# All output stores on one queue, the last evictions between ScalarE and VectorE swapped, and new instruction orders, in a transducer joint kernel

## The chip, the cores and the metric

The kernel runs on one core of a Trainium2 chip. A core has a matrix engine (TensorE, PE in the profile), which reads its weights by a separate instruction (PEld); a vector engine (VectorE, DVE); a scalar engine (ScalarE, ACT); GpSimd (POOL); and SyncE (SP), which here does nothing but issue transfers. Engines take their instructions in order and wait for each other through semaphores. The metric is the device time in microseconds of one execution; the lower the better.

## The reference

Two strided five-tap convolutions with a gelu after each, two projections, a tanh over every pair of time step and label step, and an output projection:

```python
h = sum_i einsum("btc,cd->btd", xp[:, i:i+T], w1[i])       # x is 2 x 4000 x 512, 5 taps
h = gelu(h)[:, ::2]                                         # 2 x 2000 x 512
f = sum_i einsum("btc,cd->btd", hp[:, i:i+T1], w2[i])
f = gelu(f)[:, ::2]                                         # 2 x 1000 x 512
fe = f @ w_f;  ge = g @ w_g                                 # g is 2 x 8 x 512
j = tanh(fe[:, :, None, :] + ge[:, None, :, :])             # 2 x 1000 x 8 x 512
out = j @ w_o                                               # 2 x 1000 x 8 x 512, bf16
```

The last product is the largest: 16,000 rows of 512 by a 512 x 512 matrix, with one tanh for each of its 8.2 million inputs.

## The kernel before

**Convolutions.** Each convolution computes three neighbouring outputs from products of sums and differences of inputs and of weights, so that there are fewer products (`Triple`, `Unit`, steps `s1` to `s5`). The sums of the inputs ("planes", "r", "t2" and so on) are made by VectorE, with some scalings by ScalarE or VectorE (`scaled`, lines 608 and 609); the weight sums are made in `w1part` and `w2part`. A `Unit` is one block of 128 output channels. TensorE has the products, ScalarE moves accumulators out (`sd`, `hT`, `fT`, line 451), VectorE combines (lines 602 and 446).

**The joint stage**, from about 130 us on. The 16,000 rows are 125 tiles of 128. Four neighbouring tiles by all 512 columns are taken as a 2 x 2 block product with seven products in place of eight (class `Seven`, 28 of them, methods `p1` to `p7`): four sums of the tanh values go to `ss` (method `sums`, line 1091, each 128x512, VectorE or GpSimd), four products are kept in `sn` (method `keep`, lines 560 on ScalarE and 561 on VectorE) or added to what was kept while they are moved out to `og` (line 446 on VectorE). The remaining tiles are direct products (class `Plain`), moved out to `ost`. The tanh itself runs on ScalarE, 1,000 columns at a time, into the rings `jT` and `jX` (line 451), ahead of the products. The convolution work of the second batch is mixed into the first part of this stage.

**Evictions.** `evict(None, ...)` may be done by ScalarE or VectorE: it is a "flex" operation, whose engine is the one in whose order list its number stands. The four sums of a `Seven` are flex too, between VectorE and GpSimd.

**Order.** All operations are numbered as the program makes them (0 to 1644). `ORDER` holds, for each engine, the list of its operations' numbers, written as differences from one to the next. A planner (`Plan`) works out from the tiles which operation must wait for which, and emits each engine's list in its order with the waits. So a change of `ORDER` moves work in time and, for flex operations, between engines; what is computed stays.

**Stores.** `store` and `store2` write finished tiles to HBM (lines 1037 and 1027), all from SyncE's queue but two at the end, issued by ScalarE.

**The end.** The last `Seven` is tiles 118 to 121. Behind its product 3 come, in TensorE's order: product 7, the plain tile 122, the first 384 columns of tile 124, product 4, tile 123 in two halves of 256 columns (method `halves`), and the last 128 columns of tile 124. The four last evictions and stores:

```python
for t, eng in ((2 * r, "act"), (2 * r + 1, "sp")):     # Seven.stores(1, True): tiles 120 and 121
Plain(plains[1]).halves("dve", "sp")                    # tile 123
end.part(slice(3 * P, NT), "act", "act")                # tile 124, last 128 columns
```

So ScalarE evicts product 4 into `og`, issues the store of tile 120, evicts the last 128 columns, and issues their store; the instructions stand in this order in its list.

Of the kernel before, what the change touches and what calls it, by code (L numbers as in the profile page):

```python
# [12 lines left out]
P = 128  # L13
# [2 lines left out]
ORDER = {  # L16
    "pe": """
# [13 lines left out]
        1 6 3 3 1 4 2 3""",  # L31
    "act": """
# [8 lines left out]
        91 -68 101 -95 96 -83 -8 25 -3 32 -23 25 -36 16 8 3 14 6 5 9 3 10 6 21 -8 14 10 3 10 6 10 3 8 6 6 3 12 7 1 8 1""",  # L41
    "dve": """
# [9 lines left out]
        -13 19 18 74 -52 -13 20 16 -9 6 -27 43 7 6 2 19 -7 13 15 -3 9 8 2""",  # L52
    "pool": """
        1 42 1 -42 1 1 1 15 218 1 -217 258 -252 253 8 89 174 150 1 54 -2 1 -31 33 33 2 -1 38 -36 35 40 -38 37 34 2 33
        -32 33 32 -30 31 1 1 33 1 28 1 1 28 155 -154 1 27 2 -1 33 -31 32 1 28 2 -1 31 -29 30 1 26 37 -36 37 1 1 33 34
        -33 34 -32 33 1 29 2 -1 33 2 -1 33 -31 32 1 34 2 35 2 27 -26 27 1 1 24 1 28 -26 29""",
    "sp": """
        6 2 1 1 1 1 1 1 1 1 1 1 1 2 2 1 1 1 1 2 1 1 1 1 1 248 1 1 1 1 1 1 2 1 1 1 1 1 254 1 1 145 3 33 33 4 1 1 30 4 33
        4 1 1 33 4 31 4 1 1 29 4 29 4 1 1 29 4 25 4 1 1 25 4 25 4 1 1 27 4 27 4 1 1 25 4 25 4 1 1 19 1 11 4 21 11 4 19
        11 4 17 11 1 1 4 17 11 1 1 4 17 11 4 1 1 19 11 4 21 1 11 4 25 4 23 1 1 4 23 4 19 1 1 7 3 3 5 5""",  # L60
}


# [252 lines left out]
def bass_standalone__seq2seq_rnn_t_joint__speech_kernel(  # L316
# [36 lines left out]
    NT = 512  # L353
# [4 lines left out]
    with ExitStack() as es:  # L358
# [659 lines left out]
        def store2(jt, src, key):  # L1018
            lo = jt * P
            if lo // T2 != (lo + 2 * P - 1) // T2:  # L1020
                for t in range(2):
                    store(jt + t, lambda a, b, t=t: src(a, b, t), key)
                return
            b, u, t = lo // T2 // U, lo // T2 % U, lo % T2
            s = src(0, P, slice(0, 2))
            dst = out[b, t:t + 2 * P, u, :].rearrange("(t p) d -> p t d", p=P)
            pl.dma("sp", lambda e: e.dma_start(dst, s.ap), (s,), (), sem_of(key), 4 * P * P * 4)

        def store(jt, src, key, eng="sp", cl=slice(0, NT)):
            lo = c0 = jt * P  # L1030
            while lo < c0 + P:
                vv = lo // T2
                n = min((vv + 1) * T2, c0 + P) - lo
                b, u, t = vv // U, vv % U, lo % T2
                s = src(lo - c0, lo - c0 + n)
                dst = out[b, t:t + n, u, cl]
                pl.dma(eng, lambda e, s=s, dst=dst: e.dma_start(dst, s.ap), (s,), (), sem_of(key), 2 * n * P * 4)  # L1037
                lo += n
# [30 lines left out]
        class Seven:  # L1069
# [60 lines left out]
            def stores(self, r, split=False):  # L1130
                key = ("s", self.n % len(og), r)
                if not split:
                    store2(self.jt + 2 * r, lambda a, b, t: self.o.rows(a, b, 2 * r + t if isinstance(t, int) else slice(2 * r, 2 * r + 2)), key)
                    return
                for t, eng in ((2 * r, "act"), (2 * r + 1, "sp")):
                    store(self.jt + t, lambda a, b, t=t: self.o.rows(a, b, t), key + (eng,), eng)

            def p1(self):
# [94 lines left out]
        plains = [j for j in range(ntile) if not any(q <= j < q + 4 for q in jts)]  # L1233
# [5 lines left out]
        for i, q in enumerate(seven):  # L1239
# [3 lines left out]
            r = []  # L1243
# [25 lines left out]
        end = Plain(plains[2])  # L1269
        end.part(slice(0, 3 * P), "dve", "sp")  # L1270
        seven[-1].p4(True)
        Plain(plains[1]).halves("dve", "sp")
        end.part(slice(3 * P, NT), "act", "act")

        pl.emit(block, [(s[0], s[1]) for s in sems.values()])

# [27 lines left out]
```

## Time and profile before

| | |
|---|---|
| median of 3 runs | 252.02 us (251.9 to 252.15) |
| profiled execution, its own time | 251.77 us |
| its span, first to last instruction | 249.9 us |
| granted TensorE clock | 0.999 |
| PE / PEld busy | 243.4 us / 182.9 us |
| DVE / ACT / POOL busy | 207.8 / 196.8 / 100.6 us |
| HBM read / written | 7.60 MB / 16.38 MB |

The page of the profile gives the busy time of each engine, then the same in 40 slices of 6.25 us; the chain that ended last follows the execution back from its end, at each step to what released it. The timeline lists single instructions, merged where they follow each other, with the idle time before them in brackets. An instruction is written as its tiles, out<-in. `SPq` and `ACTq` are the issuing of transfers by these engines, which does not count as busy time. One busy share hides something here: two evictions that follow each other on an engine overlap, so what one more of them costs is the distance of their starts and not their duration.

### The profile page before, as it was taken

How to read it: one execution, taken by the hardware profiler on the slowest of the kernel's cores; microseconds unless marked ns; L12 is line 12 of the kernel's file. 1: busy time of each engine (PE TensorE's matmuls, PEld its weight loads, DVE VectorE, ACT ScalarE, POOL GpSimd, SP SyncE). 2: the span in 40 equal slices, each digit the busy share in tenths (PEclk: the TensorE clock that was granted, in tenths of full speed). 3: DMA queues.
4: the chain of work that ended last, by engine and by line, in shares of the span. 5: the costliest groups of instructions: out<-in, count | busy, mean ns of one | idle time of the engine just before them, and what ended most of it. 6: DMA issues, size and time to landing. Idle time of an engine off the chain costs nothing.

```text
span 249.9 us, 5265 instructions
## 1 busy us (share of the span) xinstructions
PE 243.4 (97%) x1938; PEld 182.9 (73%) x1944; DVE 207.8 (83%) x369; ACT 196.8 (79%) x338; POOL 100.6 (40%) x107
## 2 busy tenths in 40 slices
PE   7999999999999999999999999999999999999992
PEld 3979976666666666666557887777888877878872
DVE  1799996967999993996857989769999999996962
ACT  4787868458795575533799999999999999997661
POOL 1000000000000000000008998969899999998510
PEclk9999999999999999999999999999999999999999
DMA  7999999999000070000001142232453656455465
GB/s 243 295 216 180 175 182 172 188 161 357 8 3 0 0 244 12 0 3 0 1 3 42 64 150 84 88 111 99 147 171 122 198 160 211 132 192 163 146 204 165
DMA packets 54871, 31.83 MB, mean 127 GB/s; under 512 B 31902, under 2 KB 54590, under 8 KB 54846
## 3 DMA queue, kind: packets, MB, share of 16 engines
q1 hardware_dynamic: 54558, 31.34, 47.7%
q8 instruction: 15, 0.25, 0.5%
q10 hardware_dynamic: 288, 0.16, 0.2%
q14 instruction: 10, 0.08, 0.1%
HBM read 7.60 MB, written 16.38 MB: 96 GB/s over the span
## 4 chain that ended last, share of the span: by engine, by line
PE 88%; ACT 5%; DMA 2%; DVE 1%; issue 1%; ACTq 1%; SPq 0%; DVEq 0%
PE acc L459 88%; ACT jT L451 2%; DMA w_sb<-in_w_dram 2%; ACT og L560 1%; ACT sn L560 1%; ACT jX L451 1%; ACTq L1037 1%; DVE og L446 1%; DVE sn L561 0%; DVE og L561 0%; PE acc L596 0%; SPq L486 0%; ACT ost L451 0%; DVEq L277 0%; ACTq L277 0%
## 5 line engine op out<-in xcount | busy, mean ns | idle before, releaser
L446 DVE TENSOR_TENSOR og<-acc,sn 128x512 bf16<-128x512 f32 x84 | 54.9, 680 | 6.6 <-PE acc L459 6.4
L451 ACT ACTIVATE jT<-feT,geT 128x1000 bf16<-128x1000 f32 (+5 forms) x60 | 57.4, 1015 | 0.3 <-DVE feT L446 0.3
L1091 POOL TENSOR_TENSOR ss<-jT 128x512 f16<-128x512 bf16 x34 | 39.4, 1176 | 35.2 <-DVE ss L1091 33.4
L459 PE MATMUL acc<-tw,ss 128*128 128x256 f16 x336 | 46.4, 273 | 0.0
L459 PE MATMUL acc<-row,w_sb 128*128 128x334 bf16 (+2 forms) x224 | 39.0, 297 | 0.0
L459 PEld LDWEIGHTS acc<-tw,ss 128*128 128x128 f16 x336 | 32.4, 98 | 7.5 <-ACT sn L560 0.5
L459 PE MATMUL acc<-wo_sb,jT 128*128 128x256 bf16 (+1 forms) x205 | 33.3, 283 | 0.2
L560 ACT ACTIVATE sn<-acc 128x512 f32<-128x512 f32 x49 | 30.3, 626 | 3.0 <-PE acc L459 2.8
L451 ACT ACTIVATE hT<-acc 128x334 bf16<-128x334 f32 (+3 forms) x36 | 15.4, 432 | 16.6 <-PE acc L459 16.0
L459 PEld LDWEIGHTS acc<-row,w_sb 128*128 128x128 bf16 x224 | 21.3, 97 | 9.2 <-DVE acc L602 0.7
L561 DVE COPY sn<-acc 128x512 f32<-128x512 f32 x35 | 23.8, 683 | 4.5 <-PE acc L459 4.2
L451 ACT ACTIVATE sd<-acc 128x334 f32<-128x334 f32 (+2 forms) x48 | 20.6, 432 | 6.3 <-PE acc L459 4.9
L459 PEld LDWEIGHTS acc<-wo_sb,jT 128*128 128x128 bf16 x208 | 20.3, 98 | 5.0
L443 POOL MEMSET hT<- 128x8 bf16 (+2 forms) x6 | 0.8, 148 | 55.2 <-ACT hT L451 42.9
L1091 POOL TENSOR_TENSOR ss<-ss,jT 128x512 f16<-128x512 f16 x18 | 21.0, 1172 | 2.7 <-DVE ss L1091 2.3
L1091 POOL TENSOR_TENSOR ss<-jT,ss 128x512 f16<-128x512 bf16 x17 | 20.0, 1177 | 2.1 <-DVE ss L1091 2.1
L446 DVE TENSOR_TENSOR row<-row 128x1336 bf16<-128x1336 bf16 (+2 forms) x24 | 18.9, 803 | 0.0
L602 DVE SCALAR_TENSOR_TENSOR acc<-acc,sd 128x334 f32<-128x334 f32 (+2 forms) x24 | 11.7, 486 | 8.1 <-PE acc L459 8.0
L451 ACT ACTIVATE jX<-feT,geT 128x1000 bf16<-128x1000 f32 (+3 forms) x20 | 18.2, 956 | 0.0
L459 PE MATMUL acc<-xp,w_t 128*128 128x334 bf16 (+1 forms) x96 | 17.6, 305 | 0.0
L459 PE MATMUL acc<-hT,w_t 128*128 128x334 bf16 x96 | 17.6, 304 | 0.0
L459 PE MATMUL acc<-wo_sb,ss 128*128 128x256 bf16 x112 | 17.3, 273 | 0.0
(130 smaller groups left out, 469.7 us busy)
## 6 DMA issues: line engine op xcount, KB each, us to landing
out_dram<-og SPq DMA_DIRECT2D x42, 256.0 KB, 2.2
w_sb<-in_w_dram SPq DMA_DIRECT2D x10, 512.0 KB, 5.9
out_dram<-og SPq DMA_DIRECT2D x14, 128.0 KB, 2.0
out_dram<-ost SPq DMA_DIRECT2D x10, 128.0 KB, 2.0
xr<-in_x_dram SPq DMA_DIRECT2D x1, 512.0 KB, 3.6
wf_sb<-in_w_f_dram SPq DMA_DIRECT2D x1, 512.0 KB, 4.1
wg_sb<-in_w_g_dram SPq DMA_DIRECT2D x1, 512.0 KB, 5.2
wo_sb<-in_w_o_dram SPq DMA_DIRECT2D x1, 512.0 KB, 7.6
```

Of the source, the lines that this page charges most:

```text
L443: pl.op("pool", lambda e: e.memset(v.ap, 0.0), (), (v,))
L446: pl.op(eng, lambda e: e.tensor_tensor(out=o.ap, in0=a.ap, in1=b.ap, op=op), (a, b), (o,), 0.02 + 2.14e-3 * o.ap.free_size() if eng == "po ...
L451: pl.op("act", lambda e: e.activation(o.ap, i.ap, func, scale=scale, bias=0.0 if bias is None else bias.ap), rd, (o,), o.ap.free_size() * ...
L459: ins = e.matmul(o.ap, lhsT=l.ap, rhs=r.ap, start=start and n == 0, stop=stop and n == len(pairs) - 1, skip_group_check=not check)
L560: pl.flex({"act": (lambda e: e.activation(o.ap, v.ap, ACT.Copy), 0.05 + n * 0.833e-3), "dve": (lambda e: e.tensor_copy(out=o.ap, in_=v.ap) ...
L561: "dve": (lambda e: e.tensor_copy(out=o.ap, in_=v.ap), 0.065 + n * 1.04e-3)}, (v,), (o,))
L602: pl.op(eng, lambda e: e.scalar_tensor_tensor(out=o.ap, in0=a.ap, scalar=f, in1=b.ap, op0=ALU.mult, op1=add), (a, b), (o,), vec_cost(o, (a ...
L1037: pl.dma(eng, lambda e, s=s, dst=dst: e.dma_start(dst, s.ap), (s,), (), sem_of(key), 2 * n * P * 4)
L1091: fn = lambda e, o=S[i], x=x, y=y, op=op: e.tensor_tensor(out=o.ap, in0=x.ap, in1=y.ap, op=op)
```

## The change

1. `Seven.stores(1, True)`: the store of tile 120 is issued by SyncE, ahead of that of tile 121.
2. Tile 123's two halves are evicted by ScalarE, not VectorE; the store stays with SyncE.
3. Tile 124's last 128 columns are evicted by VectorE, not ScalarE, and stored by SyncE, not ScalarE. ScalarE issues no transfer any more.
4. `ORDER` is new for all five engines. TensorE's list has another operation at 101 of its 696 places, the first at the 59th; SyncE's differs only in its last four entries. The flex operations that change engines, counted by number from the two lists: in the joint stage 24 evictions of 128x512 go from VectorE to ScalarE and 16 the other way, 18 sums go from GpSimd to VectorE and 16 the other way; in the convolutions five scalings go from ScalarE to VectorE and three small ones the other way.

```diff
 ORDER = {
     "pe": """
...
-        15 1 -6 1 14 1 7 1 8 -12 -12 1 12 5 1 12 -5 1 5 2 1 2 1 8 1 4 1 -8 20 19 -29 3 1 16 19 25 -47 1 -17 20 19 -28 1
+        15 1 -6 1 14 1 -8 1 14 1 2 -6 1 6 7 -2 3 4 1 2 1 2 1 8 5 -7 8 -5 17 -10 29 -26 1 16 19 -22 1 46 -63 20 19 -28 1
...
     "act": """
...
-        91 -68 101 -95 96 -83 -8 25 -3 32 -23 25 -36 16 8 3 14 6 5 9 3 10 6 21 -8 14 10 3 10 6 10 3 8 6 6 3 12 7 1 8 1""",
+        42 -24 26 -21 8 3 42 2 -24 -9 14 8 3 44 -37 13 -11 1 24 3 -26 42 -10 23 -93 101 6 10 3 10 6 10 3 8 6 6 3 12 7 4
+        2""",
...
     "sp": """
...
-        11 4 17 11 1 1 4 17 11 1 1 4 17 11 4 1 1 19 11 4 21 1 11 4 25 4 23 1 1 4 23 4 19 1 1 7 3 3 5 5""",
+        11 4 17 11 1 1 4 17 11 1 1 4 17 11 4 1 1 19 11 4 21 1 11 4 25 4 23 1 1 4 23 4 19 1 1 7 3 3 4 1 5 3""",
 }
...
-                for t, eng in ((2 * r, "act"), (2 * r + 1, "sp")):
+                for t, eng in ((2 * r, "sp"), (2 * r + 1, "sp")):
                     store(self.jt + t, lambda a, b, t=t: self.o.rows(a, b, t), key + (eng,), eng)
...
         seven[-1].p4(True)
-        Plain(plains[1]).halves("dve", "sp")
-        end.part(slice(3 * P, NT), "act", "act")
+        Plain(plains[1]).halves("act", "sp")
+        end.part(slice(3 * P, NT), "dve", "sp")
```

More of the change, by code (lines that the diff above doesn't have):

```diff
@@ L23 @@
         -5 1 8 43 1 -39 1 12 -8 1 10 -8 1 20 1 2 1 2 1 16 -7 1 2 1 4 6 1 2 1 2 1 2 1 2 1 6 1 2 1 3 1 5 1 4 1 2 1 2 1 2 1
[7 rows of a table removed]
-        1 6 3 3 1 4 2 3""",
-    "act": """
[8 rows of a table removed]
-        91 -68 101 -95 96 -83 -8 25 -3 32 -23 25 -36 16 8 3 14 6 5 9 3 10 6 21 -8 14 10 3 10 6 10 3 8 6 6 3 12 7 1 8 1""",
-    "dve": """
[9 rows of a table removed]
-        -13 19 18 74 -52 -13 20 16 -9 6 -27 43 7 6 2 19 -7 13 15 -3 9 8 2""",
[7 rows of a table added]
+        -11 1 12 1 2 1 2 1 8 1 -4 1 6 3 3 1 4 2 3""",
+    "act": """
[9 rows of a table added]
+        2""",
+    "dve": """
[9 rows of a table added]
+        19 42 -15 3 -13 21 -2 18 6 3 6 7 7 14 -7 6 3 20 6 -13 16 18 -7 13 15 -3 9 13""",
     "pool": """
-        1 42 1 -42 1 1 1 15 218 1 -217 258 -252 253 8 89 174 150 1 54 -2 1 -31 33 33 2 -1 38 -36 35 40 -38 37 34 2 33
-        -32 33 32 -30 31 1 1 33 1 28 1 1 28 155 -154 1 27 2 -1 33 -31 32 1 28 2 -1 31 -29 30 1 26 37 -36 37 1 1 33 34
-        -33 34 -32 33 1 29 2 -1 33 2 -1 33 -31 32 1 34 2 35 2 27 -26 27 1 1 24 1 28 -26 29""",
+        1 42 1 -42 1 1 1 15 218 1 -217 258 -252 253 8 89 174 150 22 33 -2 1 2 33 2 35 -34 35 40 -2 35 -34 35 -33 69 31
+        -32 34 -32 33 32 2 27 -26 27 1 1 28 2 -1 154 -125 1 31 2 -1 30 2 -1 30 -28 29 1 1 26 37 -36 37 -35 36 1 33 2 -1
+        33 2 -1 31 2 -1 33 2 -1 33 2 -1 37 -1 36 -34 36 1 26 2 -1 2 53 -28 29 -27 29""",
     "sp": """
```

48 rows, old and new, of the table ORDER are left out of this document.

## The prediction

> **What bounds the kernel now.** I read the page first: busy time by engine, and the slices.
>
> ```profile
> span 249.9 us, 5265 instructions
> PE 243.4 (97%) x1938; PEld 182.9 (73%) x1944; DVE 207.8 (83%) x369; ACT 196.8 (79%) x338; POOL 100.6 (40%) x107
> ...
> PE   7999999999999999999999999999999999999992
> ...
> ACT  4787868458795575533799999999999999997661
> ```
>
> PE is busy in every slice but parts of the first and the last. Its instructions stay the same, so the body can hardly get shorter; it can only get longer, where a new order lets PE wait. ScalarE is full from about 130 us to 220 us. The second view is the chain that ended last, its final pieces (start us, us, what):
>
> ```profile
> 223.56 18.78 PE acc L459 x163
> 242.34 0.05 issue
> 242.39 1.91 PE acc L459 x11
> 244.30 0.02 issue
> 244.32 0.60 ACT og L560
> 244.93 0.02 issue
> 244.95 2.44 ACTq L1037
> 247.39 0.04 issue
> ...
> 247.50 0.28 ACT ost L451
> ```
>
> Up to 244.3 us the chain is PE's work. Then it leaves PE and runs through ScalarE: the eviction of product 4, the issue of its store, which takes 2.44 us, and the last small eviction behind it. The timeline of that stretch shows what the others had done by then:
>
> ```profile
> 244.12 1.26 PE L459 MATMUL acc<-wo_sb,jX 128*128 128x256 bf16 x12
> ...
> 244.76 0.86 DVE L565 CAST ost<-acc 128x256 bf16<-128x256 f32 x2 [0.32 <-PE acc L459]
> 244.94 0.38 SPq L1037 DMA_DIRECT2D out_dram<-og  x1
> ...
> 245.65 0.33 SPq L1037 DMA_DIRECT2D out_dram<-ost  x1
> 247.50 0.28 ACT L451 ACTIVATE ost<-acc 128x128 bf16<-128x128 f32 x1 [2.58 <-DMA out_dram<-ost]
> 247.80 0.34 ACTq L1037 DMA_DIRECT2D out_dram<-ost  x1
> ```
>
> PE has ended at 244.12 + 1.26 = 245.38. The last 128 columns lie ready from then on, and are touched at 247.50 because ScalarE is still issuing. From the last issue to the end of the span it is 249.9 - 247.80 = 2.1 us. So 4.5 us lie behind PE's end, about 2.1 of them idle for one long issue.
>
> **The end, part by part.** The stores of the tile `og` (count, then ns min/median/max) price an issue:
>
> ```profile
> L1027 SPq DMA_DIRECT2D out_dram<-og x42: 372/394/502, 141.2 to 243.4; - x42
> L1037 SPq DMA_DIRECT2D out_dram<-og x40: 318/418/2207, 143.1 to 244.9; - x40
> ...
> L1037 ACTq DMA_DIRECT2D out_dram<-og x1: 2444/2444/2444, 244.9 to 244.9; - x1
> ...
> DMA to landing us min/median/max: 1.5/2.1/4.3
> ```
>
> The new end, step by step, with PE's end held:
> - Product 4's eviction stays on ScalarE, 244.32 to 244.92.
> - Tile 123's halves: the first is ready at 244.76 (VectorE began there, released by PE). ScalarE's evictions of 512 columns follow each other at about 0.48 us (rows below), so the first half starts at 244.80. No row has 256 columns on ScalarE; 128 take 0.28 us and 512 take 0.60, so 256 lie between and I take 0.39 by proportion. The second half is ready some 0.44 us after the first (half of VectorE's 0.86, which went with PE), runs from about 245.2 to 245.6.
> - The last 128 columns on VectorE, freed of the halves, start at 245.4. Their price lies under the 0.43 of a half; at 0.28, as on ScalarE, they are out at 245.7. Cover: this and the halves end side by side, and a store of SyncE's queue is still ahead of both.
> - SyncE gets two more issues, and both stand in front of or behind others. Tile 120: 244.94 to 245.32. Tile 121, which started at 244.94, now 245.34 to 245.72. Tile 123 waited for its halves until 245.65 and now starts at about 245.75. The last 128 columns follow at 245.75 + 0.33 = 246.1.
> - From there 2.1 us as before: the end is at 248.2, against 249.9. **The gain is 1.7 us.**
>
> Bounds of this term: with issues of 0.33 and a landing 0.1 shorter, 248.0 (gain 1.9); with issues of 0.50 (the largest of the 42) and a landing that queues behind three 128 KB stores, 2.5 us, it is 249.1 (gain 0.8). The new waits have little behind them: behind SyncE's wait for tile 123 stands only the last store, and behind ScalarE's halves nothing.
>
> Here a rule of the Trainium skill speaks against the change. The page "DMA: Bandwidth & Descriptors", section "Issuing engines are not separate DMA queues", says that transfers started from several engines run on the same 16 DMA engines, so that a second queue saves only the time of issuing. By it, giving up the second queue buys nothing and costs one issue of 0.38 us: 252.4 us. The two rows at 244.94 and 244.95 disagree: the same kind of store, 0.38 us on SyncE and 2.44 us on ScalarE, side by side. I go by the rows.
>
> **The body.** Stages by 10 us (PE, PEld, DVE, ACT, POOL busy), and rows that price a moved eviction:
>
> ```profile
> 10.00:30.00 20.00, 20.00 (x217) 17.79 (x215) 19.82 (x50) 17.54 (x37) 0.48 (x4) 1.00 1.09 203
> ...
> 200.00:210.00 10.00, 9.95 (x81) 7.92 (x82) 9.54 (x16) 10.00 (x14) 10.00 (x10) 1.00 0.57 183
> 210.00:220.00 10.00, 9.95 (x82) 7.82 (x81) 10.00 (x18) 10.00 (x14) 10.00 (x9) 1.00 0.47 154
> 220.00:230.00 10.00, 9.95 (x84) 7.96 (x83) 7.83 (x14) 8.98 (x18) 9.30 (x9) 1.00 0.56 180
> 230.00:240.00 10.00, 10.00 (x94) 8.60 (x92) 8.67 (x14) 7.00 (x14) 5.97 (x6) 1.00 0.51 168
> ```
>
> ```profile
> 198.62 2.47 DVE L446 TENSOR_TENSOR og<-acc,sn 128x512 bf16<-128x512 f32 x4
> ...
> 221.78 0.68 ACT L560 ACTIVATE ost<-acc 128x512 bf16<-128x512 f32 x1
> 222.25 0.69 ACT L560 ACTIVATE sn<-acc 128x512 f32<-128x512 f32 x1
> ...
> 223.83 0.83 ACT L451 ACTIVATE jX<-feT,geT 128x152 bf16<-128x152 f32 x2
> ...
> 230.10 1.15 POOL L1091 TENSOR_TENSOR ss<-jX 128x512 f16<-128x512 bf16 x1
> ```
>
> On ScalarE two evictions start 222.25 - 221.78 = 0.47 us apart, on VectorE (2.47 - 0.68) / 3 = 0.60. Of the moved evictions 24 go to ScalarE and 16 away: net 8, or 8 x 0.48 = 3.8 us more for ScalarE and 4.8 less for VectorE, which takes two more sums. The cover is ScalarE's idle time from 220 to 240 us, 20 - 8.98 - 7.00 = 4.0 us. The evictions that were issued from 200 to 222 us give 11 to ScalarE and 2 away: 9 x 0.48 = 4.3 us, in a stretch where ScalarE is full. It then runs its tanhs later: the last ended at 223.83 + 0.83 = 224.7 us, and the sums that use the last tiles were made at 230.1, so 5.4 us were to spare. Net of 1.1 us, it holds; that is thin but enough. SyncE's stores in the body keep their order.
>
> The convolutions move five scalings to VectorE, where 10 to 30 us is 19.82 of 20 us full, and three small ones to ScalarE:
>
> ```profile
> 15.47 0.37 DVE L609 TENSOR_SCALAR row<-xa 128x832 bf16<-128x832 bf16 x1
> ...
> 25.06 1.32 ACT L608 ACTIVATE row<-xp 128x1352 bf16<-128x1352 bf16 x1
> ```
>
> Three lie in that stretch. 832 columns take 0.37 us there, so the two of 1,352 take at most 1352/832 x 0.37 = 0.60 each and the one of 512 at most 0.37: 1.6 us at most on VectorE, against 2 x 1.32 and more saved on ScalarE. In the new list two other steps of that size (`ti` of the second block, and its second plane) stand behind its `t2`, which PE needs first; that covers it. I take 0 for both; if nothing covers, it costs 1.6.
>
> What PE already loses to late evictions can be read from its waits in 6 to 245 us (total, times, longest):
>
> ```profile
> PEld acc L459 <- DVE acc L602: 0.7, 3, 0.2
> PEld acc L459 <- ACT sn L560: 0.5, 2, 0.3
> ```
>
> Each is 0.3 us at most, and weights load ahead of the products, so a new order can win some tenths and lose as much: body 0, from -0.4 to +3.8 (the 8 evictions with no cover).
>
> **Sum.** 249.9 - 1.7 = 248.2 us of span. Outside the span lie 251.77 - 249.9 = 1.9 us; the profiled execution would take 250.1. The median of the runs stands 0.25 above the profiled one, so 250.3 us.
>
> **Rivals.**
> A, ScalarE becomes the bound of the joint stage: the tanhs or the kept products come late, and PE waits for them. For: 9 more evictions in a stretch with no idle time. Against: the 5.4 us of lead. It decides from 1.7 / 0.48 = 3.5 uncovered evictions on; with 4 to 8 of them 252.2 to 254.1 us, slower in most of that.
> B, ScalarE is held at 244.95 whatever instruction stands there:
>
> ```profile
> q14 instruction: 1, 0.01, 0.3%
> ```
>
> This row, of transfers from 244 to 250 us, is one fetch of instructions. If it held ScalarE until 247.4, the halves would start at 247.45 and 247.9, end at 248.2, and the stores go at 248.25 and 248.6: the end is at 250.7, 0.8 us later, 252.8 us, slower. Against: no other row of ScalarE's shows such a stop.
> C, the 2.44 us goes with the store, because the DMA engines are still busy with the four before it. Then SyncE's queue takes it: 244.94 + 2.44, two more issues, the last at 248.1, the end at 250.2: 252.3 us, no change. For: SyncE has an issue of 2.21 us too. This is the mechanism that the skill's rule of shared engines would suggest. Against: SyncE's issues at 244.94 and 245.65, in the same backlog, took 0.38 and 0.33.
>
> **Chances.** A change within 0.2% (0.5 us) is about what a measurement of this kernel can't tell from none. The forecast, with the body within half a us, 0.62: 249.8 to 251.1, its own range. The end as said, but 0.8 to 1.7 us lost in the body, 0.14: 251.1 to 252.0, of which 0.08 are below 251.5. A 0.11, B 0.07, C 0.06. Faster: 0.62 + 0.08 = 0.70. Same: the other 0.06 and C's 0.06, 0.12. Slower: A and B, 0.18. The range, 249.6 to 252.4, holds the first two cases and C, and leaves out B and most of A, some 0.16.
>
> **What would show it.** No issue by ScalarE, and SyncE's last four issues at 0.3 to 0.4 us each, the last at about 246.1; PE's last product at 245.4 as now; the chain going from PE through ScalarE's or VectorE's last eviction straight to the store. If PE's last product comes later than 246.0, the body has paid (A: waits of PEld for `sn` or `jT` after 200 us). If a store at the end still takes over 2 us it is C, and if ScalarE's halves start at 247 it is B.

## The result: 251.51 us against 252.03, and the profile after

The changed kernel takes 251.51 us (median of 20 runs) against 252.03 us for the one before (20 runs on the same chip). The ratio is 0.9979, 95% interval 0.9972 to 0.9986: faster by 0.5 us, where 1.7 us were forecast. Each ratio in this document sets undisturbed executions against undisturbed executions of before that were made beside them. Line numbers are one higher than before. The page after, its busy line and ScalarE's slices:

```profile
span 249.8 us, 5245 instructions
...
PE 244.5 (98%) x1937; PEld 182.4 (73%) x1944; DVE 209.8 (84%) x364; ACT 197.9 (79%) x345; POOL 98.3 (39%) x105
...
ACT  4677669458886575633699999999999999999872
```

The span is 0.1 us shorter, and TensorE is busy 1.1 us more. ScalarE's row of nines is one slice longer and has an 8 behind it where before has a 7: it is full until some 231 us, before until 225. The timeline of the end (start us, us, engine, line, instruction):

```profile
245.29 1.26 PE L460 MATMUL acc<-wo_sb,jX 128*128 128x256 bf16 x12
245.49 0.60 ACT L561 ACTIVATE og<-acc 128x512 bf16<-128x512 f32 x1 [0.49 <-PE acc L460]
245.99 0.76 ACT L452 ACTIVATE ost<-acc 128x256 bf16<-128x256 f32 x2
246.12 0.87 SPq L1038 DMA_DIRECT2D out_dram<-og  x2
246.59 0.29 DVE L566 CAST ost<-acc 128x128 bf16<-128x128 f32 x1 [0.98 <-PE acc L460]
247.03 0.95 SPq L1038 DMA_DIRECT2D out_dram<-ost  x2
```

TensorE ends at 245.29 + 1.26 = 246.55 us, before at 245.38: 1.17 us later. From there to the end of the span it is 249.84 - 246.55 = 3.28 us (the span to two places), before 4.57. So the end gains 1.29 us, and what stands ahead of it loses 1.17. The chain that ended last shows two places of that loss:

```profile
1.65 6.39 DMA w_sb<-in_w_dram
...
234.85 0.61 ACT sn L561
...
235.49 0.59 DVE og L447
236.08 0.05 issue
236.13 7.38 PE acc L460 x66
...
246.59 0.29 DVE ost L566
```

The first is the load of the weights at the start: it differs from one execution to the next, and no engine's list has reached a changed place there. To leave it out I take TensorE's weight loads one by one (the program has the same 1,944 in every kernel here) and subtract the start of the n-th in before from that in the other kernel. Three kernels below that have before's lists in the body (`tail_only`, `one_store_sp`, `six_more`) lag by 0.27, 0.47 and 0.31 us at load 1200 and by at most 0.02 us more at load 1920, so a lag that grows on the way comes from the lists. This lag, in us, for the kernels that are compared in it (loads counted from 0):

| weight load no. | in before at | after | sum_behind | relief_again | two_to_scalar |
|---|---|---|---|---|---|
| 40 | 7.7 | 0.39 | 0.52 | 0.14 | 2.51 |
| 1200 | 156 | 0.35 | 0.46 | 0.11 | 2.55 |
| 1280 | 167 | 0.53 | 0.65 | 0.31 | 2.73 |
| 1760 | 224 | 0.50 | 0.65 | 0.44 | 2.99 |
| 1840 | 233 | 0.82 | 0.99 | 0.46 | 3.99 |
| 1920 | 242 | 1.17 | 0.95 | 0.42 | 3.95 |

Of after's 1.17 us, 0.39 are the start's. The body costs 1.17 - 0.39 = 0.78 us: nothing in the convolutions (up to 156 us), 0.2 at 161 us (a wait of 0.3 us for one of ScalarE's evictions), and the rest from 230 to 236 us. 1.29 - 0.78 = 0.51 us, which is the measured gain. TensorE's waits from 156 to 246 us, first before, then after (total, times, longest):

```profile
PEld acc L459 <- ACT sn L560: 0.5, 2, 0.3
PEld acc L459 <- DVE sn L561: 0.2, 1, 0.2
```

```profile
PEld acc L460 <- ACT sn L561: 1.2, 6, 0.3
PEld acc L460 <- DVE og L447: 0.8, 2, 0.5
PEld acc L460 <- DVE sn L562: 0.2, 1, 0.2
```

### The profile page after: what moved, and what is told of

Its sections match the earlier page's. It is cut to its first block, busy times and chain, and to the rows that moved or that the text cites. A ratio compares the mean times of both kernels' runs of the same rounds, so it can differ in the third digit from the quotient of the medians.

```text
span 249.8 us, 5245 instructions
## 1 busy us (share of the span) xinstructions
PE 244.5 (98%) x1937; PEld 182.4 (73%) x1944; DVE 209.8 (84%) x364; ACT 197.9 (79%) x345; POOL 98.3 (39%) x105
## 4 chain that ended last, share of the span: by engine, by line
PE 94%; DMA 3%; DVE 1%; SPq 0%; issue 0%; ACT 0%; DVEq 0%
PE acc L460 94%; DMA w_sb<-in_w_dram 3%; DVE og L447 0%; DVE sn L562 0%; ACT sn L561 0%; PE acc L597 0%; SPq L478 0%; SPq L487 0%; DVE ost L566 0%; DVEq L278 0%
## 5 line engine op out<-in xcount | busy, mean ns | idle before, releaser
L452 ACT ACTIVATE jT<-feT,geT 128x1000 bf16<-128x1000 f32 (+5 forms) x60 | 60.8, 1079 | 0.3 <-DVE feT L447 0.3
L1092 POOL TENSOR_TENSOR ss<-jT 128x512 f16<-128x512 bf16 x36 | 41.8, 1174 | 42.6 <-DVE ss L1092 36.4
L561 ACT ACTIVATE sn<-acc 128x512 f32<-128x512 f32 x52 | 35.1, 694 | 1.9 <-PE acc L460 1.9
L562 DVE COPY sn<-acc 128x512 f32<-128x512 f32 x32 | 21.7, 684 | 3.4 <-PE acc L460 3.3
L1092 POOL TENSOR_TENSOR ss<-ss,jT 128x512 f16<-128x512 f16 x17 | 20.3, 1195 | 1.9 <-DVE ss L1092 1.4
L452 ACT ACTIVATE jX<-feT,geT 128x1000 bf16<-128x1000 f32 (+3 forms) x20 | 19.7, 1031 | 0.0
L561 ACT ACTIVATE og<-acc 128x512 bf16<-128x512 f32 x25 | 17.2, 688 | 0.9 <-PE acc L460 0.9
L460 PE MATMUL acc<-xp,w_x 128*128 128x334 bf16 (+1 forms) x96 | 17.1, 305 | 0.0
```

What stands on the lines that cost most here:

```text
L452: pl.op("act", lambda e: e.activation(o.ap, i.ap, func, scale=scale, bias=0.0 if bias is None else bias.ap), rd, (o,), o.ap.free_size() * ...
L460: ins = e.matmul(o.ap, lhsT=l.ap, rhs=r.ap, start=start and n == 0, stop=stop and n == len(pairs) - 1, skip_group_check=not check)
L561: pl.flex({"act": (lambda e: e.activation(o.ap, v.ap, ACT.Copy), 0.05 + n * 0.833e-3), "dve": (lambda e: e.tensor_copy(out=o.ap, in_=v.ap) ...
L562: "dve": (lambda e: e.tensor_copy(out=o.ap, in_=v.ap), 0.065 + n * 1.04e-3)}, (v,), (o,))
L1092: fn = lambda e, o=S[i], x=x, y=y, op=op: e.tensor_tensor(out=o.ap, in0=x.ap, in1=y.ap, op=op)
```

## Experiments

Two questions: does the body's loss come from ScalarE's full list (rival A in small), and why was ScalarE's issue of 2.44 us gone? Order lists are shown decoded, as operation numbers; "before" and "after" are the two kernels.

### The two halves of the change alone

`tail_only` is before with the new end, and `body_only` is after with before's end:

```diff
 tail_only: the lists of before, and
-  "act": ... 1627 1634 1635 1643 1644    "dve": ... 1630 1638 1640    "sp": ... 1631 1636 1641
+  "act": ... 1627 1634 1638 1640         "dve": ... 1630 1643         "sp": ... 1631 1635 1636 1641 1644
 body_only: the lists of after, and
-  "act": ... 1627 1634 1638 1640         "dve": ... 1630 1643         "sp": ... 1631 1635 1636 1641 1644
+  "act": ... 1627 1634 1635 1643 1644    "dve": ... 1630 1638 1640    "sp": ... 1631 1636 1641
```

(1635 and 1636 are the stores of tiles 120 and 121, 1638 and 1640 the halves of tile 123, 1643 and 1644 the last 128 columns and their store.)

> The order lists of before, with only the new end: both last stores of the og tile and the last one of 128 columns issued by SyncE, tile 123's halves evicted by ScalarE, the last 128 columns by VectorE. If end and body add up (the end gains, the reordered body costs about 0.8 us in the joint stage), PE's last product stands at 245.4 us as in before and the time is 1.3 to 1.7 us under before, about 250.5. If instead the body cost nothing and the new end was worth only the 0.5 us that the whole change showed, it is about 251.5.

> The order lists of after up to the last six instructions, with before's end. If end and body add up, PE's last product is some 0.8 us later than in before, with the stall of PE at 235 to 236 us behind VectorE's sum, and the time is about 0.8 us above before, 252.8. If the body costs nothing (the later end of PE in the profile of after is a later transfer of w_sb at the start, by chance), it is 252.0 to 252.4, not to be told from before.

`tail_only` took 250.60 us, ratio to before 0.9933 (0.9909 to 0.9957), as expected if end and body add up. `body_only` took 251.46 us, 0.9968 (0.9949 to 0.9986): faster than before, where 0.8 us slower was expected. Its timeline shows why:

```profile
245.51 1.26 PE L460 MATMUL acc<-wo_sb,jX 128*128 128x256 bf16 x12
...
246.34 0.38 ACTq L1038 DMA_DIRECT2D out_dram<-og  x1
246.82 0.28 ACT L452 ACTIVATE ost<-acc 128x128 bf16<-128x128 f32 x1 [0.51 <-PE acc L460]
...
247.13 0.35 ACTq L1038 DMA_DIRECT2D out_dram<-ost  x1
```

This is before's end, instruction for instruction, with ScalarE's store at its old place among the same others, and the issue takes 0.38 us, not 2.44. The body has paid as expected (TensorE ends at 246.77; by the weight loads its lag grows by 0.82 us behind the start), but the end is 3.12 us long instead of 4.57. So the long issue belongs neither to ScalarE's queue as such, nor to a first transfer, nor to the stores at the end. What differs is only what stands ahead of it.

### One store moved

`one_store_sp` is before with the store of tile 120 alone moved to SyncE.

```diff
-  "act": ... 1634 1635 1643 1644    "sp": ... 1631 1636 1641
+  "act": ... 1634 1643 1644         "sp": ... 1631 1635 1636 1641
```

> Before, with only the store of tile 120 moved from ScalarE's to SyncE's queue; the last 128 columns stay with ScalarE, eviction and store. If ScalarE's long issue is that of its first transfer, the store of the last 128 columns is now the first and takes about 2.4 us from 245.8 on: 252.0 to 252.4, no gain. If the long issue belongs to the place (several stores at once, or the code of that place), the last issue takes 0.34 us and the time is 250.3 to 250.7. If SyncE's queue takes it over, one of its last issues takes over 2 us: about 252.

251.22 us, ratio 0.9955 (0.9938 to 0.9972): none of the three forecasts. The long issue moved on to ScalarE's next store, and it got shorter. The timeline, and then the transfers from 246 to 248 us by queue (packets, MB, share):

```profile
246.20 1.70 ACTq L1038 DMA_DIRECT2D out_dram<-ost  x1
```

```profile
q14 instruction: 1, 0.01, 1.5%
```

That fetch of instructions is in before too, during the long issue (the prediction's row under rival B). Counting the records of each engine in the traces, with waits, shows whose it is. Before 245 us, fetches of this size start when ScalarE has begun 68, 194 and 320 records (at 40.8, 122.7 and 187.1 us), and then 448 (at 245.9): about every 128. In after they come at 66, 192, 321 and 450, the last at 240.2 us, because ScalarE's list there has 13 more records ahead of the end. Each trace also has six other fetches of this size; the next experiment shows that these four are ScalarE's. This gave a new theory, F: an issue of ScalarE's that falls together with the fetch of its own instructions is long.

### Moving the fetch, not the stores

`six_more` is before with six activations of one column added at the start of ScalarE's list, which write a buffer that nothing reads. `store_at_fetch` and `store_beside` are after with one store of the body issued by ScalarE, at its fetch and shortly behind it.

```diff
 six_more
+        spare = at("spare", [6], FP32)
...
-        act(warm[0:1], warm[1:2], ACT.Gelu_apprx_tanh)
+        wo, wi = warm[0:1], warm[1:2]
+        more = [spare[k:k + 1] for k in range(6)]
...
+            ins = e.activation(wo.ap, wi.ap, ACT.Gelu_apprx_tanh, scale=1.0, bias=0.0)
+            for v in more:
+                ins = e.activation(v.ap, wi.ap, ACT.Gelu_apprx_tanh, scale=1.0, bias=0.0)
...
 store_at_fetch
-  "act": ... 1592 1600 1606 ...         "sp": ... 1570 1593 1597 ...
+  "act": ... 1592 1593 1600 1606 ...    "sp": ... 1570 1597 ...
 store_beside
-  "act": ... 1592 1600 1606 1612 ...         "sp": ... 1593 1597 1616 ...
+  "act": ... 1592 1600 1606 1597 1612 ...    "sp": ... 1593 1616 ...
```

> Before, with its order and its end, and six activations of one column more at the very start of ScalarE's list (they write a spare buffer). Theory F: ScalarE's long issue is a DMA issue that falls together with the fetch of ScalarE's own instructions, which comes at about the 447th record of its list. Six records more bring the fetch to about 242 us, between evictions; the issue at 245 takes 0.38 us, as in the kernel with after's body and before's end, the tail from PE's end to the end of the span is 3.1 us in place of 4.6, and the time is 250.4 to 250.9. Rival N: the long issue has to do with the end itself (the first transfer of ScalarE, the stores at once): it stays at 2.4 us, and the time is that of before, 252.0 to 252.4.

> After, with one 256 KB store of the body (tiles 112 and 113, SyncE at 240.5 us) issued by ScalarE, right behind the eviction that ends at 240.3, so at about the 449th record of its list and at its fetch of instructions (240.2). Theory F: this issue takes 1.5 to 2.5 us, far from the end of the kernel. Rival N: it takes 0.4 to 0.5 us, as SyncE's did.

> After, with the next 256 KB store (tiles 114 and 115, SyncE at 242.1 us) issued by ScalarE, some five records behind the fetch, again its first transfer. Theory F: 0.35 to 0.5 us. If a first transfer is long by itself: 1.5 to 2.5 us.

`six_more` took 250.54 us, ratio 0.9950 (0.9936 to 0.9963). The timeline of its end:

```profile
244.43 1.26 PE L461 MATMUL acc<-wo_sb,jX 128*128 128x256 bf16 x12
...
245.26 0.38 ACTq L1048 DMA_DIRECT2D out_dram<-og  x1
...
246.04 0.35 ACTq L1048 DMA_DIRECT2D out_dram<-ost  x1
```

Its transfers from 242 to 244 us hold the fetch, those from 245 to 247 none:

```profile
q14 instruction: 1, 0.01, 1.0%
```

Six instructions whose results nothing uses, and the end is 3.11 us long. They also show whose the fetches are: the four that were put down to ScalarE come earlier (35.7, 114.6, 185.4 and 243.0 us, at 63, 187, 321 and 449 records), and the other six stay within 0.4 us of their places in before. In the other two kernels, run once each for their traces (252.11 and 251.79 us), the timeline shows ScalarE's rows around the fetch, in `store_at_fetch`:

```profile
239.32 0.59 ACT L561 ACTIVATE og<-acc 128x512 bf16<-128x512 f32 x1
239.94 1.46 ACTq L1028 DMA_DIRECT2D out_dram<-og  x1
241.45 1.09 ACT L561 ACTIVATE sn<-acc 128x512 f32<-128x512 f32 x2 [1.53 <-PE acc L460]
```

and in `store_beside`, with the transfers of its stretch 239.5 to 240.5 us below:

```profile
239.96 0.60 ACT L561 ACTIVATE sn<-acc 128x512 f32<-128x512 f32 x1
240.74 0.60 ACT L561 ACTIVATE sn<-acc 128x512 f32<-128x512 f32 x1 [0.17 <-PE acc L460]
241.90 0.42 ACTq L1028 DMA_DIRECT2D out_dram<-og  x1
```

```profile
q14 instruction: 1, 0.01, 2.9%
```

With the fetch in flight the issue takes 1.46 us, 1.9 us behind it 0.42, and an eviction beside the same fetch takes its usual 0.60. All of ScalarE's first issues together, by the number of ScalarE's records begun before them:

| kernel | issue at | ScalarE's record | fetch's transfer at | issue took |
|---|---|---|---|---|
| before | 244.95 | 447 | 245.87 | 2.44 |
| one_store_sp | 246.20 | 448 | 246.38 | 1.70 |
| store_at_fetch | 239.94 | 449 | 239.85 | 1.46 |
| store_beside | 241.90 | 451 | 240.01 | 0.42 |
| six_more | 245.26 | 453 | 243.04 | 0.38 |
| body_only | 246.34 | 460 | 240.43 | 0.38 |

F holds in all six. In the three long cases the issue ends 1.0 to 1.2 us behind the end of the fetch's transfer (at 247.39, 247.90 and 241.40 us, against 246.18, 246.87 and 240.27), wherever it began; so its length goes with when the fetch comes. `tail_only` has the fetch in the same stretch, at 246.16 us, but no issue by ScalarE: SyncE's two from 246.15 on take 0.96 us, as in after. In `one_store_sp` SyncE's issue at 246.34 took 0.66 us in place of 0.33, which stays unexplained. What in the chip ties fetch and issue together these runs don't show.

### The body: one sum, and how full ScalarE is

At 236.1 us TensorE waits for an add to `og`. The timeline of after shows what VectorE did ahead of it:

```profile
233.60 0.61 ACT L452 ACTIVATE jX<-feT,geT 128x152 bf16<-128x152 f32 x1
...
234.31 1.16 DVE L1092 TENSOR_TENSOR ss<-jX 128x512 f16<-128x512 bf16 x1
...
235.39 1.28 DVE L447 TENSOR_TENSOR og<-acc,sn 128x512 bf16<-128x512 f32 x2
```

ScalarE's last tanh ends at 234.21 (before at 224.7), so the sum of its tile, which the change gave to VectorE, starts at 234.31, takes 1.16 us, and holds up the add. `sum_behind` puts it behind the add. `relief_again` does that too and gives three evictions back to VectorE; `two_to_scalar` does that and gives two more to ScalarE.

```diff
 sum_behind, relief_again, two_to_scalar
-  "dve": ... 1540 1554 1547 1553 ...
+  "dve": ... 1540 1547 1554 1553 ...
 relief_again
-  "act": ... 1375 1355 1363 ... 1389 1397 1400 ... 1431 1434 1476 ...
+  "act": ... 1375 1363 ... 1389 1400 ... 1431 1476 ...
-  "dve": ... 1360 1378 ... 1394 1412 ... 1428 1448 ...
+  "dve": ... 1360 1355 1378 ... 1394 1397 1412 ... 1428 1434 1448 ...
 two_to_scalar
-  "dve": ... 1394 1412 1415 ... 1428 1448 1451 ...    "act": ... 1400 1442 ... 1434 1476 ...
+  "dve": ... 1394 1415 ... 1428 1451 ...              "act": ... 1400 1412 1442 ... 1434 1448 1476 ...
```

> After, with VectorE's sum from jX (S26, first pair), which took 1.16 us at 234.3, moved two places down its list, behind the add to og that PE waits for at 236.1. If that place is what cost PE its 0.39 us, the wait goes and the time is 0.3 to 0.4 us under after, about 251.1. If ScalarE is late anyway and another wait takes its place (the sum itself, needed later by PE), it is within 0.1 us of after, 251.5.

> After, with VectorE's sum behind the add as before, and three of the evictions that the change gave to ScalarE (at 213.4, 217.8 and 222.0 us) given back to VectorE, into its idle time of 0.5 to 0.9 us there. If the waits of PE at 230 to 232 us (0.28 us) come from ScalarE's full list, ScalarE is some 1.4 us earlier, its last tanh ends at about 232.8 in place of 234.2, the waits are gone, and the time is 0.2 to 0.3 under the kernel with the sum alone moved. If VectorE takes over the lateness, waits of PE for its results appear at 215 to 226 and the time is equal or above.

> The same kernel as the one with three evictions given back to VectorE, once more, for a profile whose stretches can be set beside those of the kernel with the sum alone moved. If ScalarE's full list makes PE's waits at 230 to 232 us, PE's lag behind before grows by less than 0.1 us from 224 to 242 us, where it grew by 0.30 with the sum alone moved (0.65 to 0.95). If VectorE takes the lateness over, the lag grows by as much, at places where PE waits for VectorE.

> The kernel with VectorE's sum behind the add, and two more evictions (at 218.8 and 222.7 us) on ScalarE in place of VectorE, as before had them. If ScalarE's full list is what PE waits for, ScalarE is some 1 us later from 223 to 234 us, and PE's lag grows by 0.7 to 1.3 us from 224 to 242 us in place of 0.30; the time is 0.4 to 1.0 us above the kernel with the sum alone moved, 251.8 to 252.4. If ScalarE's lateness there does not matter, it is 251.4.

| kernel | median us | before beside it | ratio to before | 95% |
|---|---|---|---|---|
| after | 251.51 | 252.03 | 0.9979 | 0.9972 to 0.9986 |
| sum_behind | 251.43 | 252.27 | 0.9961 | 0.9944 to 0.9978 |
| relief | 250.93 | 251.73 | 0.9963 | 0.9950 to 0.9977 |
| relief_again | 250.81 | 252.02 | 0.9951 | 0.9937 to 0.9966 |
| two_to_scalar | 252.18 | 252.02 | 1.0001 | 0.9992 to 1.0011 |

`relief` and `relief_again` are the same kernel; the trace is the second's. With the sum moved, the lag no longer grows from 233 to 242 us (0.99 to 0.95, where after has 0.82 to 1.17): that wait is gone, and no other took its place; in time, the intervals of the two overlap. Nor can the relief, forecast to be 0.2 to 0.3 us faster, be told from `sum_behind` in time; `two_to_scalar` is slower than it beyond both intervals. TensorE's waits from 156 to 246 us, in `sum_behind`, `relief_again` and `two_to_scalar`:

```profile
PEld acc L460 <- ACT sn L561: 1.4, 7, 0.3
PEld acc L460 <- DVE og L447: 0.3, 1, 0.3
```

```profile
PEld acc L460 <- ACT sn L561: 0.7, 3, 0.3
PEld acc L460 <- DVE sn L562: 0.5, 2, 0.4
```

```profile
PEld acc L460 <- ACT sn L561: 2.3, 8, 0.5
PEld acc L460 <- DVE sn L562: 0.4, 2, 0.2
PEld acc L460 <- DVE og L447: 0.3, 1, 0.3
```

Two evictions more or three fewer on ScalarE, and TensorE's waits for it go from 1.4 us to 2.3 or 0.7. From 224 to 242 us the lag grows by 0.30 in `sum_behind`, by 0.96 with two more, and by -0.02 with three fewer. (The lag of 2.51 us with which `two_to_scalar` starts is that of its one traced execution, whose granted clock was 0.50 from 7 to 10 us; from 220 to 242 us it was 1.00.) A part of the relief comes back as waits for VectorE (0.17 us of lag between 214 and 224 us, counted in the trace), and the last tanh ended only 0.5 us earlier than in `sum_behind`, not 1.4; without the difference of the two starts, 0.38 us, it is 0.15. Busy times from 220 to 240 us (PE, PEld, DVE, ACT, POOL) show how near the edge after stands; ScalarE has 1.5 us left of 20, where before had 4.0:

```profile
220.00:230.00 10.00, 9.90 (x80) 7.82 (x81) 9.18 (x15) 10.00 (x18) 6.19 (x6) 1.00 0.49 158
230.00:240.00 10.00, 9.78 (x87) 7.83 (x86) 8.48 (x15) 8.51 (x15) 9.13 (x9) 1.00 0.52 169
```

## Why the prediction was right in sign and too large

- **The 2.44 us.** The step that read this issue as the price of ScalarE's queue, from the two rows at 244.94 and 244.95, got the cause wrong. Its size and its place on the path were right: without it the same end is 3.12 us long in place of 4.57. But it goes too with edits that only move ScalarE's fetch away from its issues, six idle instructions among them; the new order of the body alone already did that. So in this change the moved stores added nothing: the new end is 3.28 us long after PE, before's end without the collision 3.12. That the time fell, as forecast, was to this extent luck: the right two microseconds were named for a wrong reason.
- **The rule of the Trainium skill.** I set aside the section "Issuing engines are not separate DMA queues" of the Trainium skill's page "DMA: Bandwidth & Descriptors", by which a second queue saves only the time of issuing. The runs agree with it: with no fetch in the way, giving up ScalarE's queue costs 3.28 - 3.12 = 0.16 us. That is from single traces, and holds the swap of the last evictions too; over all traces here the new end is 3.26 to 3.39 us long and the old one 3.11 and 3.12, so it is 0.1 to 0.3 us. The 252.4 us that I worked out by the rule was wrong because the rule speaks of the issues, and the 2.44 us was no issue's own price.
- **Rival B** had the right row (the fetch of instructions) and the wrong rule: it is not whatever stands there that is held. Evictions pass beside a fetch at 0.60 us; in three of three cases an issue did not. My "against" (no other row of ScalarE's shows such a stop) overlooked that ScalarE had no other issue. Rival C's backlog is out: `body_only` and `six_more` have the same backlog and 0.38 us.
- **SyncE's issues** were taken at 0.33 to 0.38 us. Two and two took 0.87 and 0.95, some 0.45 each. The last issue ended 247.98 - 246.55 = 1.43 us behind PE's end instead of 246.43 - 245.38 = 1.05, so the term of 1.7 us measured 1.3. ScalarE's halves (0.76 for both, directly behind product 4) and VectorE's 128 columns (0.29) came as forecast.
- **The body at 0** is the term that failed: it cost 0.78 us. The convolutions did cost nothing. In the joint stage the cover that I named was gone: I put ScalarE's tanhs 4.3 us later, within 5.4 us of lead, and the last one came 9.5 us later (234.2 against 224.7). The step that failed is the count of 9 evictions. It took only those that changed engine from 200 to 222 us, but as ScalarE is full there, what delays a tanh is all that stands ahead of it in the new list. Ahead of the last tanh ScalarE has 58 evictions by line 560 before and 77 (line 561) after: 24 came from VectorE, 13 went to it, and 8 that ScalarE had done behind that tanh were moved ahead of it. 19 x 0.48 = 9.1 us, and 0.4 are the start's. Nearly all of ScalarE's idle time was spent, so its evictions came late for TensorE, and the sum, moved to VectorE, could start only where it blocked an add. That is rival A's mechanism, at 0.8 us, below the 1.7 from which it was to decide. The run with two more evictions on ScalarE shows how steep it is: behind the start its lag is 3.95 - 2.51 = 1.44 us, against 0.95 - 0.52 = 0.43, and the gain over before is gone.
- **What would show it:** PE's last product after 246.0 was named as the sign that the body had paid. It came at 246.55, of which 0.39 were the start's.

Before's own lists with either end free of the collision beat both kernels: 250.60 us (`tail_only`) and 250.54 us (`six_more`), which can't be told apart from each other, nor from `relief_again`.

## What to carry to other kernels

An instruction that takes six times as long as its neighbours of the same kind is a question, not a price: look which transfers run beside it, instruction fetches among them, before a sum is built on its going away. An order that fills an engine to the last microsecond has used up the lead that hid its lateness, and what it then delays is found by following one late result to the next engine's list. Take out of two traces what differs by chance (here the start) before the stages are compared, and test the halves of a change apart: here the new end alone gained three times what the whole did.

## What the hardware showed that was not expected

ScalarE's fetches of instructions come about every 128 records, and an issue of a transfer by ScalarE beside one took 1.46 to 2.44 us instead of 0.38 to 0.42, in three of three placements; evictions beside one were not slowed. SyncE's issues may be held by larger fetches (by the count of records they would be TensorE's): in before, from 143.1 us on, three issues take 2.96 us together (one of them 2.2), and the transfers from 143 to 144 us hold a fetch of twice the size:

```profile
143.10 2.96 SPq L1037 DMA_DIRECT2D out_dram<-og  x3
```

```profile
q8 instruction: 1, 0.02, 11.2%
```

That was seen, not tried. Its two other output stores over 0.7 us (1.28 us at 176.45, 0.80 at 205.92) lie beside such fetches too, but so does its issue at 205.06, which took 0.39. In the body a long issue can be hidden or not: in `store_at_fetch` TensorE's lag grows by 0.87 us from 235 to 242 us, in `store_beside`, with an issue of 0.42 us, by 0.36, and in after not at all. At the end of before the long issue cost 4.57 - 3.12 = 1.45 us.
